# Top-32 attention and a low-rank mixer on one core: first heads masked through a gap from the scalar engine

## The chip, the cores and the metric

The kernel runs on one core of a Trainium2 chip. A core has five engines that work side by side and wait for each other through semaphores. TensorE (PE) multiplies matrices into the accumulator memory PSUM. VectorE (DVE) does elementwise work, finds the eight largest of a row (MAX8) and replaces them (MATCH_REPLACE8). ScalarE (ACT) computes a function of a scaled and shifted input. GpSimd (POOL) does elementwise work on SBUF, and SyncE (SP) issues the transfers. Each engine takes its instructions in the order of the program. The metric is the device time of one execution in microseconds, smaller being better.

## The reference

Eight batches of eight heads go through attention that keeps the 32 largest scores of each row. The result goes through a mixer with a low-rank step along the sequence and two layers along the channels.

```python
B, H, S, D = 8, 8, 576, 64            # top_k = 32
scores = (q @ k.T) / sqrt(D)
kth    = np.partition(scores, -top_k)[..., -top_k]
scores = np.where(scores >= kth, scores, -1e9)
attn   = np.exp(scores - scores.max(-1))
attn   = attn / (attn.sum(-1) + 1e-09)
x      = (attn @ v)                    # (B, S, H*D) after a transpose

h   = (x.T @ U @ V).T                  # rank 32
u   = x + h
out = u + np.maximum(u @ w_ch1, 0) @ w_ch2     # 512 -> 2048 -> 512
```

All of it is in 32-bit floats.

## The kernel before

Two heads make a pair; there are `NPAIR` = 4 pairs in a batch and 32 in all. The 576 rows of a head are four tiles of 128 rows and a tail of 64; in the tail the two heads share the 128 partitions. One tile of one pair is a step: `CH` = 5 steps to a pair and 160 steps, where step `n` is pair `g, t = divmod(n, CH)`. The first batch is the steps 0 to 19 (`ALONE` = 20). From step 20 the mixer of the batch before is fed in small pieces, `fill()`, between the steps of the attention. The mixer of the last batch comes when no attention is left.

Scores are four matmuls and copies out of PSUM. A tail takes four copies of 64 rows:

```python
S2 = attn.tile([P, 2 * (S + TAIL)], F32, tag="Ssb", bufs=3)
scs = [ps_s.tile([P, 2, 512], F32, tag="sc") for _ in range(2)]
for i, sc in enumerate(scs):
    for h in range(2):
        nc.tensor.matmul(                                              # L274
            sc[slice(0, n) if t < NT else half(h), h, 0:HALF],
            lhsT=qkT[half(h), 0, cols(t)],
            rhs=qkT[half(h), 1, i * HALF : (i + 1) * HALF], ...)
if t == NT:
    for i, sc in enumerate(scs):
        for h in range(2):
            nc.scalar.copy(S2[half(h), i*HALF : (i+1)*HALF], sc[half(h), h, 0:HALF])   # L284
    S2s[g, t] = [S2[:, 0:S]]
    return
...                                       # full tiles: three copies, L293 to L295
```

`front` is the work of a step on one tile: for each of the two heads (chunks), four times the eight largest of a row. The last of the 32 is the threshold. The first head is then masked on DVE: its exponential has been computed early, and one instruction compares with the threshold, multiplies and sums. The second head is masked on POOL before its exponential: what is below the threshold gets a huge negative number added. Each `yield` is a place where the main loop goes on with other work.

```python
order = (1, 0) if n == 2 else (0,)
for c in order:
    ms[c] = first[:, c]
    nc.vector.max(ms[c], curs[c])                                      # L320
yield
pooled = n == 2 and (g, t) != (NPAIR - 1, NT - 1)
for i in range(1, TOPK // 8):
    if i == 1:
        nc.scalar.mul(nmax[:, 0:n], first[:, 0:n, 0], -SCALE)          # L325
        for c in range(1 if pooled else n):
            weigh(chunks[c], Es[c], nmax[:, c : c + 1])                # Exp, L300
    for c in order:
        ...
        nc.vector.match_replace(nxt, ms[c], curs[c], NEG)              # L330
    for c in order:
        ...
        nc.vector.max(ms[c], curs[c])                                  # L334
    yield
if pooled:
    nc.gpsimd.tensor_scalar(Es[1], chunks[1], ms[1][:, 7:8], NEG, ALU.is_lt, ALU.mult)  # L337
    nc.gpsimd.tensor_tensor(chunks[1], chunks[1], Es[1], ALU.add)      # L338
for c in range(1 if pooled else n):
    nc.vector.scalar_tensor_tensor(out=Es[c], in0=chunks[c],           # L340
        scalar=ms[c][:, 7:8], in1=Es[c], op0=ALU.is_ge, op1=ALU.mult, accum_out=sums[c])
yield
if pooled:
    weigh(chunks[1], Es[1], nmax[:, 1:2], sums[1])                     # Exp, L300
yield
```

After this the weights E are transposed on PE (`turns`, L367 and L372, with copies `PT` on ACT) and multiplied with v (`values`, L403). The sums of a pair stand in `den`; at the pair's tail `inverse` adds 1e-9 and takes reciprocals on DVE:

```python
def inverse(g, lo, hi):
    den = dens[g][:, lo:hi]
    nc.vector.tensor_scalar_add(den, den, 1e-9)                        # L378
    nc.vector.reciprocal(den, den)                                     # L379
```

The main loop for the first batch (steps 1 to 18; at steps 19 and 20 an order of its own is used). `here` is the front of step n, whose first part has been issued, and `last` is that of step n - 1. `next_params(1)` loads one piece of the mixer's weights (36 pieces) and converts those loaded before, with three operations on ACT (L161 to L164), one on DVE (L171) and two on POOL (L172, L174); in the first batch there are six calls to a pair.

```python
next(turning, None); next(turning, None)      # rest of turns(n - 2)
scores(*divmod(n + 1, CH))
fill()
turning = turns(*divmod(n - 1, CH))
if n >= 2: values(*divmod(n - 2, CH))
next(here)                                    # i = 1
next_params(1)
next(turning, None)                           # first part of turns(n - 1)
fill()
next(last, None)                              # Exp of the second head of n - 1
next(ready, None)
next(here)                                    # i = 2
...
next(here)                                    # i = 3
if t == 1: next_params(1)
next(here)                                    # masks
fill()
```

From step 21 on:

```python
fill(); next(turning, None); fill(); next(turning, None); fill(); next(ready, None); fill()
values(*divmod(n - 2, CH)); scores(*divmod(n + 1, CH))
next(here, None)                              # i = 1
next_params(1)
...
fill(); next(here, None); fill()              # i = 2
turning = turns(*divmod(n - 1, CH)); next(turning, None)
fill(); next(here, None); next(last, None)    # i = 3; Exp of the second head of n - 1
if t in (1, 3): next_params(1)
next(here, None); fill()                      # masks
```

The pieces of the mixer that one `fill()` takes are set by a share, which is 0.91 of the full one up to step 42.

Of the kernel before, what the change touches and what calls it, by code (L numbers as in the profile page):

```python
# [8 lines left out]
F32 = mybir.dt.float32  # L9
U8 = mybir.dt.uint8  # L10
U32 = mybir.dt.uint32
AF = mybir.ActivationFunctionType
ALU = mybir.AluOpType
# [3 lines left out]


RESCALE = 2.0**-112

TINY = 0.4 * 2.0**-15

# [2 lines left out]
def kernel(  # L25
# [28 lines left out]
    nc = tc.nc  # L54
    B, H, S, D = q.shape
    P = 128
# [4 lines left out]
    NT, TAIL = 4, 64  # L61
    MAIN = NT * P
    HALF = S // 2
    assert S == MAIN + TAIL and D == 64 and H % 2 == 0 and C == 512 and TOPK % 8 == 0
    NPAIR = H // 2
# [7 lines left out]
    const = ctx.enter_context(tc.tile_pool(name="const", bufs=1))  # L73
# [37 lines left out]

    nudge = const.tile([P, 1], F32, name="nudge")
    nc.vector.memset(nudge, TINY)

    def rows(t):
        return P if t < NT else TAIL

    def cols(t):
        return slice(t * P, t * P + rows(t))
# [4 lines left out]
    def half(h):  # L124
        return slice(h * D, (h + 1) * D)
# [139 lines left out]
    def scores(g, t):  # L265


        qkT = qkTs[g]
        n = rows(t)
        S2 = attn.tile([P, 2 * (S + TAIL)], F32, tag="Ssb", name="Ssb", bufs=3)  # L270
        scs = [ps_s.tile([P, 2, 512], F32, tag="sc", name="sc") for _ in range(2)]
        for i, sc in enumerate(scs):
            for h in range(2):
                nc.tensor.matmul(  # L274
                    sc[slice(0, n) if t < NT else half(h), h, 0:HALF],
                    lhsT=qkT[half(h), 0, cols(t)],
                    rhs=qkT[half(h), 1, i * HALF : (i + 1) * HALF],
                    start=True,
                    stop=True,
                )  # L280
        if t == NT:
            for i, sc in enumerate(scs):
                for h in range(2):
                    nc.scalar.copy(  # L284
                        S2[half(h), i * HALF : (i + 1) * HALF], sc[half(h), h, 0:HALF]
                    )
            S2s[g, t] = [S2[:, 0:S]]
            return

        main = S2.rearrange("p (h n) -> p h n", h=2)  # L290
        last = S2[:, MAIN : MAIN + 2 * TAIL].rearrange("p (h n) -> p h n", h=2)
        copy = nc.vector.tensor_copy if g + t == 0 else nc.scalar.copy
        copy(main[:, :, 0:HALF], scs[0][:, :, 0:HALF])  # L293
        nc.scalar.copy(main[:, :, HALF:MAIN], scs[1][:, :, 0 : MAIN - HALF])
        nc.scalar.copy(last, scs[1][:, :, MAIN - HALF : HALF])  # L295
        S2s[g, t] = [S2[:, 0:S], S2[:, S : 2 * S]]

    def weigh(chunk, E, nmax, total=None):

        nc.scalar.activation(E, chunk, AF.Exp, bias=nmax, scale=SCALE, accum_out=total)  # L300

    def front(g, t):

        if t == 0:
            dens[g] = small.tile([P, 2 * NT + 1], F32, tag="den", name="den", bufs=3)
        chunks, den = S2s.pop((g, t)), dens[g]
        n = len(chunks)
        E2 = attn.tile([P, 2 * S], F32, tag="E", name="E", bufs=3)  # L310
        Es = [E2[:, c * S : (c + 1) * S] for c in range(n)]
        sums = [den[:, 2 * t + c : 2 * t + c + 1] for c in range(n)]
        probs[g, t] = E2
        curs, ms = list(chunks), [None] * n
        first = small.tile([P, 2, 8], F32, tag="first", name="first", bufs=3)
        nmax = small.tile([P, 2], F32, tag="nmax", name="nmax", bufs=4)
        order = (1, 0) if n == 2 else (0,)
        for c in order:
            ms[c] = first[:, c]
            nc.vector.max(ms[c], curs[c])  # L320
        yield
        pooled = n == 2 and (g, t) != (NPAIR - 1, NT - 1)
        for i in range(1, TOPK // 8):
            if i == 1:
                nc.scalar.mul(nmax[:, 0:n], first[:, 0:n, 0], -SCALE)  # L325
                for c in range(1 if pooled else n):
                    weigh(chunks[c], Es[c], nmax[:, c : c + 1])
            for c in order:
                nxt = attn.tile([P, S], F32, tag="rr", name="rr", bufs=3)
                nc.vector.match_replace(nxt, ms[c], curs[c], NEG)  # L330
                curs[c] = nxt
            for c in order:
                ms[c] = small.tile([P, 8], F32, tag="m8", name="m8", bufs=8)
                nc.vector.max(ms[c], curs[c])  # L334
            yield
        if pooled:
            nc.gpsimd.tensor_scalar(Es[1], chunks[1], ms[1][:, 7:8], NEG, ALU.is_lt, ALU.mult)  # L337
            nc.gpsimd.tensor_tensor(chunks[1], chunks[1], Es[1], ALU.add)  # L338
        for c in range(1 if pooled else n):
            nc.vector.scalar_tensor_tensor(  # L340
                out=Es[c],
                in0=chunks[c],
                scalar=ms[c][:, 7:8],
                in1=Es[c],
                op0=ALU.is_ge,
                op1=ALU.mult,
                accum_out=sums[c],
            )
        if t == NT:
            del qkTs[g]  # L350
        yield
        if pooled:
            weigh(chunks[1], Es[1], nmax[:, 1:2], sums[1])
        yield

    def turns(g, t):
# [18 lines left out]

    def inverse(g, lo, hi):
        den = dens[g][:, lo:hi]
        nc.vector.tensor_scalar_add(den, den, 1e-9)  # L378
        nc.vector.reciprocal(den, den)  # L379

    def values(g, t):
# [189 lines left out]
    for n in range(STEPS + 2):  # L571
        g, t = divmod(n, CH)
        if n < STEPS:
            if t == 0 and g + 1 < NP:
                load(g + 1)
            if t == 1 and g + 1 < NP:
                ready = prep(g + 1)
            fronts[n] = front(g, t)
            next(fronts[n])
        here, last = fronts.get(n, iter(())), fronts.pop(n - 1, iter(()))  # L580
        if n >= ALONE - 1 and n <= ALONE:

            list(turning)
            if n < ALONE:
                scores(*divmod(n + 1, CH))
            list(turns(*divmod(n - 1, CH)))
            if n < ALONE:
                values(*divmod(n - 2, CH))
                next(here)
            values(*divmod(n - 1, CH))  # L590
            if n < ALONE:
                inverse(g, 0, 2 * NT)
                next(here)
                mixing.append(mixed(g, 1))
                fill()
                next(here)
                next(here)
                continue
            fill()
            scores(*divmod(n + 1, CH))  # L600
            next(here)
            while mixing:
# [3 lines that stand above are left out]
            next(last, None)  # L606
            next(here)
            fill()
            next(here)
            next(here)  # L610
            fill()
            continue
        if n < ALONE:
            next(turning, None)
            next(turning, None)
            scores(*divmod(n + 1, CH))
            fill()
            if n >= 1:
                turning = turns(*divmod(n - 1, CH))
            if n >= 2:  # L620
                values(*divmod(n - 2, CH))
            next(here)
            next_params(1)
            next(turning, None)
            fill()
            next(last, None)
            next(ready, None)
            next(here)
            fill()
            if n >= 2 and (n - 2) % CH == NT:  # L630
                mixing.append(mixed((n - 2) // CH, 3))
            next(here)
            if t == 1:
                next_params(1)
            next(here)
            fill()
            continue
        fill()
        next(turning, None)
        fill()  # L640
        next(turning, None)
# [3 lines that stand above are left out]
        if n - 2 >= ALONE:  # L645
            values(*divmod(n - 2, CH))
        if n + 1 < STEPS:
            scores(*divmod(n + 1, CH))
        next(here, None)
        next_params(1)  # L650
        if n - 2 >= ALONE and (n - 2) % CH == NT:
            mixing.append(mixed((n - 2) // CH, 4))
        fill()
        next(here, None)
        fill()
        if n <= STEPS:
            turning = turns(*divmod(n - 1, CH))
        next(turning, None)
        fill()
        next(here, None)  # L660
        next(last, None)
        if t in (1, 3):
            next_params(1)
        next(here, None)
        fill()
# [33 lines left out]
```

## Time and profile before

| | |
|---|---|
| time | 1860.22 us, median of 3 runs (1859.81 to 1860.23) |
| span of the profiled run | 1861.6 us |
| PE busy | 1750.6 us, 94% |
| DVE busy | 1617.2 us, 87% |
| ACT busy | 1008.1 us, 54% |
| POOL busy | 635.7 us, 34% |

These shares are averages over a run with different stages, so they don't tell what a change in one stage is worth. The page also has the busy tenths of each engine in 40 equal slices, the groups of instructions by line, and the chain of work that ended last. The trace behind it answers for any stretch of time what each engine did and what it waited for.

### The profile page before, as it was taken

What the parts mean: (1) busy time and instruction counts of PE and PEld (TensorE: products, weight loads), DVE (VectorE), ACT (ScalarE), POOL (GpSimd) and SP (SyncE); (2) the same over time, 40 slices, a digit from 0 to 9 for tenths busy, and PEclk for the clock granted to TensorE, in tenths of its full rate; (3) what the DMA queues carried; (4) which work ended last, traced back from release to release, by engine and by line L of the source; (5) the groups of instructions that cost most, each with busy time, mean ns of one, the idle gap of its engine ahead of it and who ended that gap; (6) DMA issues with size and microseconds to landing.
All of it is one profiled execution on the core that took longest, in us unless ns stands there. A gap on an engine that the chain in (4) does not pass through costs nothing.

```text
span 1861.6 us, 29241 instructions
## 1 busy us (share of the span) xinstructions
PE 1750.6 (94%) x10528; PEld 1324.0 (71%) x10528; DVE 1617.2 (87%) x3316; ACT 1008.1 (54%) x2466; POOL 635.7 (34%) x432
## 2 busy tenths in 40 slices
PE   4565789999999999999999999999999999999999
PEld 3443556787777877788777877788777877788677
DVE  7999999999999999999999999999999999996000
ACT  4666677555655555555555555555555555554111
POOL 4556466433333332323233332332323332322000
PEclk7677799999999999999999999999999999999999
DMA  3222222101000010110001010101001010000000
GB/s 98 76 72 75 63 81 81 28 23 32 15 21 22 23 29 21 30 25 24 23 13 31 21 32 20 28 22 27 14 24 27 25 30 21 10 8 7 6 14 12
DMA packets 127296, 58.23 MB, mean 31 GB/s; under 512 B 89904, under 2 KB 124976, under 8 KB 127152
## 3 DMA queue, kind: packets, MB, share of 16 engines
q1 hardware_dynamic: 126096, 56.10, 11.3%
q8 instruction: 84, 1.38, 0.3%
q14 instruction: 60, 0.49, 0.1%
q10 hardware_dynamic: 1056, 0.26, 0.1%
HBM read 46.89 MB, written 9.44 MB: 30 GB/s over the span
## 4 chain that ended last, share of the span: by engine, by line
PE 84%; DVE 10%; ACT 4%; issue 1%; POOL 1%; DMA 0%; POOLq 0%; SPq 0%; DVEq 0%; ACTq 0%
PE mm L472 27%; PE mm L491 26%; PE sc L274 9%; PE O L403 6%; PE tp L367 6%; DVE rr L330 4%; DVE m L334 3%; PE O L390 2%; PE up L447 2%; PE O L400 1%; DVE first L320 1%; PE tp L254 1%; PE tp L519 1%; PE up L449 1%; PE tp L372 1%
## 5 line engine op out<-in xcount | busy, mean ns | idle before, releaser
L334 DVE MAX8 m<-rr 128x8 f32<-128x576 f32 x864 | 614.8, 749 | 5.5
L491 PE MATMUL mm<-hT,w 128*128 128x256 f32 (+1 forms) x2048 | 562.2, 410 | 0.0
L472 PE MATMUL mm<-uT,w 128*128 128x256 f32 (+1 forms) x2048 | 557.9, 411 | 1.5 <-ACT hT L484 1.5
L337 POOL TENSOR_SCALAR E<-Ssb,m 128x576 f32<-128x576 f32 x127 | 285.2, 2246 | 650.7 <-DVE m L334 512.7
L472 PEld LDWEIGHTS mm<-uT,w 128*128 128x128 f32 x2048 | 363.3, 190 | 108.6 <-issue 27.6
L491 PEld LDWEIGHTS mm<-hT,w 128*128 128x128 f32 x2048 | 360.5, 190 | 97.7 <-issue 22.5
L330 DVE MATCH_REPLACE8 rr<-m,rr 128x576 f32<-128x576 f32 x576 | 427.8, 743 | 0.0
L367 PE MATMUL tp<-ident,E 128*128 128x128 f32 x1152 | 184.7, 285 | 53.8 <-ACT E L300 38.7
L368 ACT COPY PT<-tp 128x512 f32<-128x512 f32 x288 | 168.4, 585 | 114.9 <-PE tp L367 113.0
L300 ACT ACTIVATE E<-Ssb,nmax 128x576 f32<-128x576 f32 x288 | 223.8, 778 | 5.9 <-POOL Ssb L338 0.7
L367 PEld LDWEIGHTS tp<-ident,E 128*128 128x128 f32 x1152 | 144.9, 147 | 106.9 <-ACT E L300 50.7
L274 PE MATMUL sc<-qkT 64*128 64x288 f32 (+1 forms) x1280 | 212.5, 454 | 0.3 <-ACT Ssb L293 0.3
L330 DVE MATCH_REPLACE8 rr<-first,Ssb 128x576 f32<-128x576 f32 x288 | 211.8, 742 | 0.0
L320 DVE MAX8 first<-Ssb 128x8 f32<-128x576 f32 x288 | 205.4, 750 | 0.9 <-ACT Ssb L295 0.9
L340 DVE SCALAR_TENSOR_TENSOR E<-Ssb,m,E 128x576 f32<-128x576 f32 x161 | 137.8, 856 | 65.6 <-ACT E L300 48.2
L338 POOL TENSOR_TENSOR Ssb<-Ssb,E 128x576 f32<-128x576 f32 x127 | 178.9, 1408 | 10.6
L484 ACT ACTIVATE hT<-mm 128x320 f32<-128x320 f32 (+1 forms) x256 | 104.4, 408 | 119.8 <-PE mm L472 119.0
L412 ACT COPY XT<-O 128x128 f32<-128x128 f32 x128 | 34.0, 266 | 215.1 <-PE O L403 215.1
L403 PE MATMUL O<-PT,va 128*64 128x128 f32 x2048 | 147.7, 289 | 0.0
L274 PEld LDWEIGHTS sc<-qkT 64*128 64x128 f32 (+1 forms) x1280 | 110.2, 187 | 51.7 <-issue 25.4
L504 DVE TENSOR_TENSOR oT<-uT,mm 128x320 f32<-128x320 f32 (+1 forms) x8 | 3.6, 455 | 146.6 <-PE mm L491 146.6
L403 PEld LDWEIGHTS O<-PT,va 128*64 128x64 f32 x2048 | 116.0, 143 | 16.8 <-issue 2.9
(73 smaller groups left out, 1484.3 us busy)
## 6 DMA issues: line engine op xcount, KB each, us to landing
raw<-in_moe_w_ch_dram SPq DMA_DIRECT2D x32, 512.0 KB, 3.7
va<-in_v_dram SPq DMA_DIRECT2D x64, 128.0 KB, 2.5
out_dram<-ob SPq DMA_DIRECT2D x64, 128.0 KB, 1.9
ld_q<-in_q_dram SPq DMA_DIRECT2D x63, 128.0 KB, 2.8
ld_k<-in_k_dram SPq DMA_DIRECT2D x63, 128.0 KB, 2.8
ld_ends<-in_q_dram SPq DMA_DIRECT2D x32, 32.0 KB, 2.2
ld_ends<-in_k_dram SPq DMA_DIRECT2D x32, 32.0 KB, 2.2
vd<-in_v_dram SPq DMA_DIRECT2D x64, 16.0 KB, 2.0
```

What stands on the lines that cost most here:

```text
L274: nc.tensor.matmul(sc[slice(0, n) if t < NT else half(h), h, 0:HALF], lhsT=qkT[half(h), 0, cols(t)], rhs=qkT[half(h), 1, i * HALF : (i + 1 ...
L300: nc.scalar.activation(E, chunk, AF.Exp, bias=nmax, scale=SCALE, accum_out=total)
L320: nc.vector.max(ms[c], curs[c])
L330: nc.vector.match_replace(nxt, ms[c], curs[c], NEG)
L334: nc.vector.max(ms[c], curs[c])
L337: nc.gpsimd.tensor_scalar(Es[1], chunks[1], ms[1][:, 7:8], NEG, ALU.is_lt, ALU.mult)
L338: nc.gpsimd.tensor_tensor(chunks[1], chunks[1], Es[1], ALU.add)
L367: nc.tensor.transpose(tp[:, j, :], E2[:, a : a + P], ident)
L368: nc.scalar.copy(PT[:, NT * h : NT * h + NT], tp)
L403: nc.tensor.matmul(O[half(h)], lhsT=va[:, h, j, :], rhs=PT[:, NT * h + j], start=False, stop=(j == NT - 1),)
L472: nc.tensor.matmul(ph[:, 0:w], lhsT=w1[:, cc, f * P : (f + 1) * P], rhs=uT[:, cc, lo:hi], start=(cc == 0), stop=(cc == NC - 1),)
L491: nc.tensor.matmul(po[:, 0:w], lhsT=w2[:, f, c * P : (c + 1) * P], rhs=hTs[f][:, 0:w], start=(f == 0), stop=(f == NF - 1),)
```

## The change

It has four parts. *First*, in the first two batches (`eased`: pairs 0 to 7, full tiles, all but tile 3 of pair 3) the first head no longer gets its mask on DVE. ACT computes, for every score, Relu of (threshold - score) x 2^96: zero for a score that is kept, a huge gap for one that is not. POOL subtracts this from the scores, and the exponential, which is then taken after the mask and no longer early, makes zero of what fell out. ACT and POOL do this at the head of the next step. *Second*, as the weights of a step are ready later, the main loop of the first batch takes the values three steps behind and the transposes a place later, and the calls for weights are spread otherwise, still six to a pair. *Third*, the addition of 1e-9 goes from DVE to ACT, for all pairs but pair 3. *Fourth*, the tail's four score matmuls go into one PSUM tile, which one copy empties. The aim is to take work off DVE while it is fully used, and to shorten ACT's part of the tails.

```diff
+WIDEN = 2.0**96
 ...
+        if t == NT:
+            sc = ps_s.tile([P, 2, 512], F32, tag="sc", name="sc")
+            for i in range(2):
+                for h in range(2):
+                    nc.tensor.matmul(sc[half(h), i, 0:HALF], ...)
+            nc.scalar.copy(S2[:, 0:S].rearrange("p (i n) -> p i n", i=2), sc[:, :, 0:HALF])
+            S2s[g, t] = [S2[:, 0:S]]
+            return
 ...
+    def eased(g, t):
+        return g < 2 * NPAIR and t < NT and (g, t) != (NPAIR - 1, NT - 1)
 ...
+        ease = eased(g, t)
         pooled = n == 2 and (g, t) != (NPAIR - 1, NT - 1)
+        early = range(0 if ease else 1 if pooled else n)
 ...
-                for c in range(1 if pooled else n):
+                for c in early:
                     weigh(chunks[c], Es[c], nmax[:, c : c + 1])
 ...
-        for c in range(1 if pooled else n):
+        for c in early:
             nc.vector.scalar_tensor_tensor(...)
         yield
-        if pooled:
-            weigh(chunks[1], Es[1], nmax[:, 1:2], sums[1])
+        if ease:
+            least = small.tile([P, 1], F32, tag="least", name="least", bufs=3)
+            nc.scalar.mul(least, ms[0][:, 7:8], WIDEN)
+            nc.scalar.activation(Es[0], chunks[0], AF.Relu, bias=least, scale=-WIDEN)
+            nc.gpsimd.tensor_tensor(chunks[0], chunks[0], Es[0], ALU.subtract)
+            yield
+        for c in order:
+            if c not in early:
+                weigh(chunks[c], Es[c], nmax[:, c : c + 1], sums[c])
+        if t == NT and g != NPAIR - 1:
+            nc.scalar.activation(den, den, AF.Identity, bias=eps)
         yield
 ...
-        nc.vector.tensor_scalar_add(den, den, 1e-9)
+        if g == NPAIR - 1:
+            nc.vector.tensor_scalar_add(den, den, 1e-9)
 ...                                          # first batch, steps 1 to 18
-            next(turning, None)
-            next(turning, None)
+            if ease:
+                next(last, None)              # gap and subtraction of n - 1
             scores(*divmod(n + 1, CH))
-            fill()
-            if n >= 1:
-                turning = turns(*divmod(n - 1, CH))
-            if n >= 2:
-                values(*divmod(n - 2, CH))
-            next(here)
-            next_params(1)
-            next(turning, None)
-            fill()
-            next(last, None)
+            if n >= 3:
+                values(*divmod(n - 3, CH))
+            list(turning)                     # all of turns(n - 2)
+            fill()
+            next(here)
+            if t < NT:
+                next_params(1)
+            fill()
             next(ready, None)
             next(here)
+            next(last, None)                  # Exp of both heads of n - 1
             ...
-            if t == 1:
+            if t in (0, 1):
                 next_params(1)
             next(here)
             fill()
+            if n >= 1:
+                turning = turns(*divmod(n - 1, CH))
 ...                                          # from step 21 on
+        if ease:
+            next(last, None)                  # gap and subtraction of n - 1, ahead of all else
         ...
             scores(*divmod(n + 1, CH))
         next(here, None)
+        if ease:
+            next(last, None)                  # Exp of both heads of n - 1
         next_params(1)
```

At step 19 the values of steps 16, 17 and 18 are taken, where before it was those of 17 and 18.

## The prediction

> **What bounds the kernel now.** I read the page's slices first, because the program has stages with different limits, then busy times cut at step boundaries, then the cost groups, then the DVE's timeline.
>
> ```profile
> PE   4565789999999999999999999999999999999999
> DVE  7999999999999999999999999999999999996000
> PEclk7677799999999999999999999999999999999999
> ```
>
> One digit is 46.5 us. For five slices DVE is full while PE is at half and its clock below full; then both are full until slice 36; at the end PE runs alone. So there are three stages. I cut them at the first MAX8 of each step: step 20, where the second batch begins and the first mixer layer starts to run, has it at 223.94 us, step 40 at 434.46, and the last DVE work of the attention ends near 1707.6. The columns are stretch, its length, then busy time with the instruction count for each engine, clock, DMA share, GB/s.
>
> ```profile
> 114.93:168.05 53.12, 32.63 (x201) 22.32 (x201) 52.04 (x111) 35.62 (x81) 31.60 (x21) 0.79 0.27 77
> 223.94:434.46 210.52, 201.29 (x1238) 148.68 (x1237) 204.91 (x425) 138.99 (x330) 106.46 (x70) 1.00 0.18 50
> 434.46:1707.60 1273.14, 1265.40 (x7865) 966.46 (x7864) 1200.61 (x2452) 709.95 (x1767) 411.84 (x263) 1.00 0.09 23
> 1707.60:1861.60 154.00, 148.64 (x667) 117.50 (x665) 3.64 (x8) 23.19 (x61) 3.21 (x4) 1.00 0.04 11
> ```
>
> The first row is one pair of heads (five steps) of batch 0: DVE 52.04 of 53.12 us, PE 32.63. Batch 0 is DVE-bound. The second is batch 1: DVE 204.91 and PE 201.29 of 210.52, both near the limit, PE with 9.23 us idle. From step 40 PE is busy 1265.40 of 1273.14 us: there PE is the bound and DVE's gaps cost nothing. The last row is PE alone. A DVE instruction is therefore worth its time in batch 0, a part of it in batch 1, and nothing later.
>
> Next the groups that the change touches (line, engine, operation, count | busy us, mean ns | idle before it).
>
> ```profile
> L340 DVE SCALAR_TENSOR_TENSOR E<-Ssb,m,E 128x576 f32<-128x576 f32 x161 | 137.8, 856 | 65.6 <-ACT E L300 48.2 <-PE tp L367 1.3 <-ACT hT L484 0.5
> L378 DVE TENSOR_SCALAR den<-den 128x9 f32<-128x9 f32 (+2 forms) x33 | 25.9, 786 | 0.3 <-ACT E L300 0.3
> L337 POOL TENSOR_SCALAR E<-Ssb,m 128x576 f32<-128x576 f32 x127 | 285.2, 2246 | 650.7 <-DVE m L334 512.7 <-PE tp L367 57.3 <-PE mm L472 40.0
> L338 POOL TENSOR_TENSOR Ssb<-Ssb,E 128x576 f32<-128x576 f32 x127 | 178.9, 1408 | 10.6
> L300 ACT ACTIVATE E<-Ssb,nmax 128x576 f32<-128x576 f32 x288 | 223.8, 778 | 5.9 <-POOL Ssb L338 0.7
> L284 ACT COPY Ssb<-sc 64x288 f32<-64x288 f32 x128 | 50.3, 393 | 15.9 <-PE sc L274 14.7
> L293 ACT COPY Ssb<-sc 128x576 f32<-128x576 f32 x127 | 81.2, 639 | 48.4 <-PE sc L274 46.8
> ```
>
> What is to be seen: the mask of a first head costs DVE 856 ns, POOL's second-head mask 2246 + 1408 ns, and a nine-column add to `den` 786 ns, more than a MAX8 over 576 columns. How much a mask really takes out of a DVE step is in the timeline, as start, duration, instruction.
>
> ```profile
> 180.59 1.02 DVE L378 TENSOR_SCALAR den<-den 128x9 f32<-128x9 f32 x1
> 181.64 0.22 DVE L379 RECIPROCAL den<-den 128x9 f32<-128x9 f32 x1
> ...
> 233.10 1.41 DVE L334 MAX8 m<-rr 128x8 f32<-128x576 f32 x2
> 234.65 0.82 DVE L340 SCALAR_TENSOR_TENSOR E<-Ssb,m,E 128x576 f32<-128x576 f32 x1
> 235.39 0.08 DVE L340 DVE_READ_ACCUMULATOR E<-Ssb,m,E 128x1 f32 x1
> 235.39 1.42 DVE L320 MAX8 first<-Ssb 128x8 f32<-128x576 f32 x2
> ```
>
> Two MAX8 that end a pass are followed elsewhere 1.33 us after their start; here the next MAX8 starts 2.29 us after (235.39 - 233.10). The mask costs 0.96 us of the step. The add costs 1.05 us (181.64 - 180.59).
>
> **What the Trainium skill says.** "SBUF — State Buffer", section "Who interferes with whom", says that GpSimd's only SBUF ports are the DVE's second pair, that a DVE tensor_scalar in a two-port mode takes the pair as an exclusive lock, and that a DVE operation with two SBUF inputs contends with GpSimd's reads. The trace agrees: the add takes from 134 to 1057 ns for nine columns or fewer and the mask from 809 to 1666 ns for one shape. MAX8 has one input, and stays between 735 and 764 ns, so more POOL work should not stretch it. "ScalarE: Activation LUTs", section "What ACT_TABLE_LOAD costs", gives an ACTIVATE with a pointer bias as 280 ns + 0.833 ns per element, by which I estimate 760 ns for the new Relu over 576 columns; the Exp of the same shape and bias measures 778 ns here, and I use that. Its section "Table sets: the hidden batching unit" has Relu in every set; the trace has one table load although Relu and Exp alternate, so no reload is to be paid. "Perfetto Trace Analysis", section "Optimizing Scalar/DVE Operations", advises fewer, larger operations because each pays a fixed access cost: four tail copies take 4 x 393 = 1572 ns, one copy of 128x576 takes 639.
>
> **The change, part by part.**
>
> *Masks leave DVE in the first two batches.* Of the 16 full tiles of batch 0 all but (3, 3) are eased: 15 x 0.96 = 14.4 us; in some steps a weight conversion stands just ahead of the mask and the mask adds only 0.73 us (190.97 to 191.70), so I take 13.7 us. Batch 1: 16 x 0.96 = 15.4 us.
>
> *The add of 1e-9 leaves DVE* for all pairs but 3. In batch 0 three of them fall (pairs 0 to 2): 3 x 1.05 = 3.1 us. In batch 1 four: 4.2 us. Later ones fall where PE is the bound: nothing.
>
> *What comes in.* ACT per eased tile: `least` (0.2 us, as `nmax`, 217 ns), Relu 0.78, and the accumulator read that the first head's Exp now has, 0.19: 1.2 us. Per pair 4 x 1.2, less 0.93 for the tail's copies, plus 0.2 for the add: 4 us. ACT goes from 35.6 to about 39.7 of a pair that shrinks to 53.1 - 4 x 0.91 - 1.05 = 48.4 us, 82%. POOL: 4 x 1.41 = 5.6, from 31.6 to 37.2, 77%. Neither fills, but both work in order, and POOL's chain for one tile is now 2.25 + 1.41 + 1.41 = 5.1 us, then two Exps of 0.97. It starts when the second head's last MAX8 is done, 0.75 us before the step ends; so both heads' E are ready some 6 us into the next step, up to 10 where two conversions (2 x 2.7 us on POOL) stand ahead. In batch 0 PE transposes E(n-1) only in step n+1 now, which leaves room; that is what the values three steps behind are for. The scores of step n+1 are copied right after the Relu and are wanted 10 us later. So I expect no new wait on DVE there.
>
> *Batch 0:* 13.7 + 3.1 = 16.8 us, all on the path.
>
> *Batch 1:* DVE's need falls from about 210.5 to 210.5 - 15.4 - 4.2 = 191 us, below PE's 201.3, which the change leaves as it is (the matmuls and the pace of the mixer's pieces per step are the same). PE becomes the bound. It could win at most its 9.2 idle us. But here E(n-1) is still transposed in the middle of step n, about 7 to 8 us in by the timeline, and in the first two pairs conversions delay POOL; ACT, which then sits at the two Exps, holds back the copies that PE's banks wait for. I put 2.5 us for that: 6.7 us won.
>
> *Tails in one copy:* 0.93 us of ACT in each of 32 tails, and one score buffer less. DVE waited 0.9 us in all for score copies to begin MAX8 and PE 0.3 us for score buffers, so it is worth nothing by itself.
>
> *Sum:* 16.8 + 6.7 = 23.5; 1860.2 - 23.5 = 1836.7, say 1837 us.
>
> **The rivals.**
>
> *A: the gain of batch 0 alone.* The late E of batch 1 makes new PE waits as long as the idle time it replaces. For it: between 230 and 480 us PE already waits 4.9 us for E by the waits, with a shorter chain. Against: PE behind DVE makes E early, not late. Time: 1860 - 17 = 1843.
>
> *B: POOL and ACT become the bound in batch 0.* ACT at 82% and POOL at 77%, in order, each waiting for the other and for weights; a stall of the Exp would reach DVE through the next scores. For it: two conversions now fall in each of the first two steps of a pair, and ACT's work there about fills a step. Against: some 7 us of slack before DVE needs a score tile. Loss of a third of the 16.8: about 1843, with rival A 1849.
>
> *C: everything comes, and more.* PE's idle time in batch 1 goes entirely, and the 3.6 us of idle at the start of batch 2, which came from a POOL add waiting behind a mask, goes with it: 16.8 + 9.2 + 3.6 = 29.6, 1831.
>
> *D: the den add matters in the long stage.* PE's 7.7 us of idle from step 40 on caps it, and that idle is not DVE's doing. I give it little.
>
> **Range and chances.** The batch 0 part is counting of instructions on a full engine and should hold within 3 us; batch 1 is open between 0 and 9 us. The range goes from just beyond C, 1829, to A with B, 1849. Faster by over 2% would need 1823 us, 37 us less, and all DVE time removed in both batches is 36.4: 4%. Slower by over 2% would need a bound in the long stage, whose instructions hardly change: 2%. Within 2%: 94%.
>
> **What would show it.** In the changed profile: step 20 begins near 207 us instead of 223.94; DVE at 96% or more of batch 0, with pairs of about 48.4 us; 130 masks of the old kind on DVE instead of 161; PE above 98% busy in the stretch of steps 20 to 39, which lasts about 204 us; the stretch from step 40 to the end as long as now, 1427 us, within 3. It is wrong if step 20 begins after 212 (then ACT or POOL has held DVE: rival B), if batch 1 lasts more than 208 us (rival A), or if the stretch after step 40 has changed by over 5 us, for which I have no mechanism.

## The result, and the profile after

The changed kernel takes 1867.35 us, median of 4 runs (1867.0 to 1867.74), against 1860.22 us before (1859.81 to 1861.27): ratio 1.0038, 95% interval 1.002 to 1.0055. It is slower by 7 us, where the prediction had 1837 us and a range from 1829 to 1849.

The first view is again the page's slices, of the kernel after.

```profile
PE   4665789999999999999999999999999999999999
DVE  7999988888999999999999999999999989996000
```

DVE has a row of 8s from slice 6 to 10, that is from about 233 to 466 us, where it had 9s. It has been relieved there, and the run didn't get shorter. Cut at step boundaries, step 20 now begins at 212.96 us and step 40 at 437.57. The rows are the pairs 1 to 3 of batch 0, all of batch 1, one pair of batch 1, and the stretch after it up to 1707.60 us; columns as before.

```profile
59.53:212.96 153.43, 96.33 (x621) 66.04 (x621) 147.38 (x306) 114.08 (x269) 104.53 (x72) 0.78 0.28 80
212.96:437.57 224.61, 202.55 (x1217) 147.29 (x1216) 189.97 (x387) 145.78 (x362) 122.93 (x83) 0.98 0.16 44
326.90:383.77 56.87, 53.02 (x321) 39.41 (x321) 46.02 (x94) 31.62 (x86) 23.55 (x16) 0.97 0.10 26
437.57:1707.60 1270.03, 1263.82 (x7864) 965.92 (x7865) 1183.87 (x2423) 690.73 (x1719) 413.77 (x264) 1.00 0.09 22
```

Batch 1 is where the time went: 224.61 us instead of 210.52. DVE's busy time there fell from 204.91 to 189.97 us, PE's is 202.55, and PE is idle for 22.1 us instead of 9.2. From step 40 to the end it is 1428.3 us against 1427.1, unchanged. Batch 0 gives 11.0 us instead of 16.8 in these two profiles.

One correction belongs here: the profiled run of the kernel before took 1863.4 us, 3 more than its median, and has 2.2 us of waiting at step 19 that a run of usual length doesn't have (experiment 9). Against that run, step 20 at 221.71, batch 0 gives 8.75 us.

The groups that answer to those shown before:

```profile
L359 DVE SCALAR_TENSOR_TENSOR E<-Ssb,m,E 128x576 f32<-128x576 f32 x130 | 117.1, 901 | 93.5 <-ACT E L310 83.0 <-PE tp L548 0.5
L310 ACT ACTIVATE E<-Ssb,nmax 128x576 f32<-128x576 f32 x288 | 222.2, 775 | 14.3 <-POOL Ssb L357 6.2 <-POOL Ssb L375 3.9
L375 POOL TENSOR_TENSOR Ssb<-Ssb,E 128x576 f32<-128x576 f32 x31 | 44.4, 1433 | 9.7 <-ACT E L374 9.5
L374 ACT ACTIVATE E<-Ssb,least 128x576 f32<-128x576 f32 x31 | 24.0, 775 | 1.0
L286 ACT COPY Ssb<-sc 128x576 f32<-128x576 f32 x32 | 20.4, 637 | 25.1 <-PE sc L279 25.1
```

31 masks have left DVE, the Relu takes 775 ns, the subtraction 1433, the tail's one copy 637: every added piece has the size that the prediction gave it. New is the idle time: DVE's remaining masks wait 83 us for the exponential, 48 before.

What PE waits for in batch 1 stands in the waits (who waited for whom: us in total, times, longest). First the kernel before, in its run of usual length, then the kernel after.

```profile
PE tp L367 <- ACT E L300: 4.9, 5, 1.8
```

```profile
PE tp L395 <- ACT E L310: 13.3, 15, 2.5
```

PE's transposes wait for the exponential in nearly every one of the 16 full tiles. One such place in the timeline of the kernel after (start, duration, engine, instruction, idle before), from the last link of POOL's chain for the tile that is then transposed:

```profile
354.42 1.42 POOL L375 TENSOR_TENSOR Ssb<-Ssb,E 128x576 f32<-128x576 f32 x1
...
359.71 1.24 PE L292 MATMUL sc<-qkT 64*128 64x288 f32 x8
...
360.51 0.64 ACT L303 COPY Ssb<-sc 128x576 f32<-128x576 f32 x1 [0.42 <-PE sc L292]
360.88 1.56 PE L501 MATMUL mm<-uT,w 128*128 128x256 f32 x6
361.05 0.54 ACT L304 COPY Ssb<-sc 128x448 f32<-128x448 f32 x1
361.47 0.28 ACT L305 COPY Ssb<-sc 128x128 f32<-128x128 f32 x1
361.63 0.23 ACT L344 ACTIVATE nmax<-first 128x2 f32<-128x2 f32 x1
361.73 0.79 ACT L310 ACTIVATE E<-Ssb,nmax 128x576 f32<-128x576 f32 x1
361.79 1.42 DVE L337 MAX8 first<-Ssb 128x8 f32<-128x576 f32 x2 [3.32 <-ACT Ssb L305]
...
362.49 0.78 ACT L310 ACTIVATE E<-Ssb,nmax 128x576 f32<-128x576 f32 x1
...
363.42 0.66 PE L395 MATMUL tp<-ident,E 128*128 128x128 f32 x4 [0.97 <-ACT E L310]
```

POOL was done at 355.84. The exponentials started 5.9 us later, because they stand on ACT behind the copies of the next scores, and those wait for PE's own score matmuls. PE then has only the 1.56 us of mixer matmuls (L501) before it needs the result, and waits 0.97 us. However far PE lags, the exponential lags with it. Meanwhile DVE, which is ahead, stands 3.32 us for scores. In 12 of the 16 tiles of batch 1 the first exponential starts 2.2 to 5.9 us after POOL's last subtraction; in the other four, all in the first two pairs, POOL was done 0.7 us or less before it, or not yet.

### The profile page after: what moved, and what is told of

Same layout as the page of the kernel before. It is cut to its first block, busy times and chain, and to the rows that moved or that the text cites. A ratio compares the mean times of both kernels' runs of the same rounds, so it can differ in the third digit from the quotient of the medians.

```text
span 1865.9 us, 29142 instructions
## 1 busy us (share of the span) xinstructions
PE 1747.5 (94%) x10528; PEld 1319.3 (71%) x10528; DVE 1576.7 (85%) x3224; ACT 1009.2 (54%) x2494; POOL 675.0 (36%) x463
## 4 chain that ended last, share of the span: by engine, by line
PE 84%; DVE 6%; ACT 4%; POOL 3%; issue 2%; DMA 0%; POOLq 0%; SPq 0%; DVEq 0%; ACTq 0%
PE mm L501 26%; PE mm L520 26%; PE sc L292 7%; PE O L432 6%; PE tp L395 6%; DVE rr L349 3%; DVE m L353 2%; PE up L476 2%; PE sc L279 2%; PE O L419 2%; ACT E L310 2%; PE O L429 1%; PE tp L258 1%; PE up L478 1%; PE tp L548 1%
## 5 line engine op out<-in xcount | busy, mean ns | idle before, releaser
L501 PE MATMUL mm<-uT,w 128*128 128x256 f32 (+1 forms) x2048 | 557.8, 411 | 0.5 <-ACT hT L513 0.5
L501 PEld LDWEIGHTS mm<-uT,w 128*128 128x128 f32 x2048 | 363.9, 190 | 107.4 <-issue 28.0
L395 PE MATMUL tp<-ident,E 128*128 128x128 f32 x1152 | 179.3, 280 | 47.5 <-ACT E L310 24.2
L395 PEld LDWEIGHTS tp<-ident,E 128*128 128x128 f32 x1152 | 140.5, 143 | 102.6 <-ACT E L310 39.7
L359 DVE SCALAR_TENSOR_TENSOR E<-Ssb,m,E 128x576 f32<-128x576 f32 x130 | 117.1, 901 | 93.5 <-ACT E L310 83.0
L292 PE MATMUL sc<-qkT 64*128 64x288 f32 x1024 | 169.6, 452 | 8.4 <-ACT Ssb L303 7.9
L432 PE MATMUL O<-PT,va 128*64 128x128 f32 x2048 | 143.7, 284 | 0.0
L536 POOL TENSOR_TENSOR oT<-oT,uT 128x320 f32<-128x320 f32 (+1 forms) x56 | 45.1, 806 | 230.9 <-ACT oT L535 230.9
L292 PEld LDWEIGHTS sc<-qkT 64*128 64x128 f32 x1024 | 93.0, 197 | 46.1 <-issue 16.6
```

The costliest lines, as they stand in the source:

```text
L292: nc.tensor.matmul(sc[:, h, 0:HALF], lhsT=qkT[half(h), 0, cols(t)], rhs=qkT[half(h), 1, i * HALF : (i + 1) * HALF], start=True, stop=True,)
L395: nc.tensor.transpose(tp[:, j, :], E2[:, a : a + P], ident)
L432: nc.tensor.matmul(O[half(h)], lhsT=va[:, h, j, :], rhs=PT[:, NT * h + j], start=False, stop=(j == NT - 1),)
L501: nc.tensor.matmul(ph[:, 0:w], lhsT=w1[:, cc, f * P : (f + 1) * P], rhs=uT[:, cc, lo:hi], start=(cc == 0), stop=(cc == NC - 1),)
```

## The experiments

Theory A: batch 1 loses through the place of the exponentials in ACT's order. Rival C: through POOL's chain, which has become longer by a subtraction. Rival B: through a part that all stages share. Theory D: the rest of batch 0's gain is lost in the weights' conversion on DVE, which waits for the port that POOL holds. Theory F came later: through the place of the tail's own exponential on ACT.

**1. Gap masks in the first batch only.**

```diff
-        return g < 2 * NPAIR and t < NT and (g, t) != (NPAIR - 1, NT - 1)
+        return g < NPAIR and t < NT and (g, t) != (NPAIR - 1, NT - 1)
```

> The changed kernel with the gap masks in the first batch only (pairs 0 to 3); the second batch masks its first heads on VectorE as before. Theory A (the loss is made in the second batch, where the two exponentials now stand behind the next scores' copies on the scalar engine, ahead of the transposes that need them): steps 20 to 39 last about 210 us as in the kernel before, the 11 us won in the first batch stay, total about 1850 us (1847 to 1853). Rival B (the loss comes from a part that all stages share, the tails' single copy or the addition on the scalar engine): total stays near 1865.

Measured: 1850.43 us (ratio to before 0.9947, 0.993 to 0.9963). Steps 20 to 39 last 210.84 us. The second batch's gap masks cost 17 us; rival B falls.

**2. The first head's exponential first.**

```diff
-        for c in order:
+        for c in range(n):
             if c not in early:
```

> The changed kernel with the two exponentials in the other order: the first head, which is transposed first, goes first. Theory A (order on the scalar engine): the first head's weights come one exponential, 0.97 us, earlier in 16 tiles of the second batch, TensorE's waits for them there fall from 13.3 us to under 5, total about 1858 us (1854 to 1861). Rival C (GpSimd's chain of three operations is what is waited for; the first head's subtraction is its last link): no gain, 1865 to 1869.

Measured: 1861.43 us (1.0001, 0.9992 to 1.0009), just above the expected range. PE's waits for the weights in batch 1 fall from 13.3 to 5.4 us, the stretch from 224.61 to 217.09. The edit also turns the order in batch 0, where step 20 begins at 214.81 us, 1.9 later. One exponential of 0.97 us earlier is worth 6 us on balance: order on ACT, not POOL, whose first-head subtraction is still the last link.

**3. Both exponentials ahead of the next scores.**

```diff
         fill()
+        if ease:
+            next(last, None)
         if n - 2 >= ALONE:
             values(*divmod(n - 2, CH))
         if n + 1 < STEPS:
             scores(*divmod(n + 1, CH))
         next(here, None)
-        if ease:
-            next(last, None)
```

> The changed kernel with both exponentials of the step before issued ahead of the values and the scores of the next step in the second batch, not behind them. Theory A: TensorE's waits for the weights in steps 20 to 39 nearly vanish (under 3 us), the stretch shrinks from 224.6 to 205-209 us, total 1848 to 1854 us. Rival C (GpSimd's chain): the scalar engine now stands at the exponentials until GpSimd is done and the score copies come later; the stretch grows, total over 1868.

Measured: 1852.82 us (0.9959, 0.9944 to 0.9974). The waits fall to 3.3 us. The stretch, 211.73 us, stays above the 205 to 209 expected. Its four pairs, from the busy times:

```profile
212.33:268.08 55.75, 48.18 (x278) 33.25 (x278) 50.18 (x104) 41.69 (x99) 39.06 (x27) 1.00 0.25 74
268.08:323.75 55.67, 50.79 (x300) 36.00 (x299) 48.71 (x100) 40.88 (x98) 38.06 (x27) 0.97 0.20 58
323.75:374.19 50.44, 50.44 (x322) 38.68 (x321) 45.74 (x94) 32.04 (x86) 22.77 (x15) 0.99 0.11 29
374.19:424.06 49.87, 49.87 (x332) 40.88 (x331) 45.62 (x94) 31.36 (x83) 21.71 (x14) 1.00 0.10 22
```

The last two are full of PE work, as predicted. In the first two, where POOL still converts weights (39 us of 56, against 22 of 50), PE is idle 12.5 us and DVE waits 10.8 us in the two tails for the exponential. There rival C has a part: ACT stood up to 2.9 us for POOL at the moved exponentials.

**4. The gap subtracted twice in the second batch.**

```diff
-            nc.gpsimd.tensor_tensor(chunks[0], chunks[0], Es[0], ALU.subtract)
+            for _ in range(2 if g >= NPAIR else 1):
+                nc.gpsimd.tensor_tensor(chunks[0], chunks[0], Es[0], ALU.subtract)
```

> The changed kernel with the gap subtracted twice on GpSimd in the second batch, so that GpSimd's chain for a tile is 1.4 us longer; the result is the same since the gap is zero for a kept score. Theory A: the chain is done before the exponentials' turn comes, total within 4 us of the changed kernel (1865 to 1871). Rival C (GpSimd's chain is waited for): up to 16 x 1.4 = 22 us more, total 1880 to 1890.

Measured: 1869.99 us (1.005, 1.0035 to 1.0065), 2.6 us more than the changed kernel for some 22 us of POOL work added to its chain. In the changed kernel, rival C is left with little.

**5. No gap masks at all, the rest of the change kept.**

```diff
-        return g < 2 * NPAIR and t < NT and (g, t) != (NPAIR - 1, NT - 1)
+        return False
```

> The changed kernel without any gap mask (VectorE masks every first head as before); the other loop order in the first batch, the addition on the scalar engine and the tails' single copy stay. If the gap masks make all of batch 0's gain but the three additions (3 us), step 20 begins near 221 us and the total is 1856 to 1859 us. Rival: the other order by itself gains or costs more than 3 us, total outside 1854 to 1862.

Measured: 1858.01 us (0.9986, 0.9979 to 0.9993), step 20 at 219.74 us. With experiment 1 this gives the first batch's gap masks 1858.0 - 1850.4 = 7.6 us for 13.7 us of DVE time.

**6. The tails' single copy alone, on the kernel before** (the tail's branch of `scores` from the diff above).

> The kernel before with the tails' single tile and copy alone. Theory: 30 us less work on the scalar engine that nothing waits for; total within 2 us of 1860. Rival: in the long stage TensorE gets the score buffers and VectorE the tails sooner, 1 us or more in each of the 32 pairs, total below 1840.

Measured: 1859.33 us (0.9991, 0.9982 to 0.9999). The medians differ by 0.7 us, and the interval allows 0.2 to 3.3.

**7. The addition of 1e-9 on ACT alone, on the kernel before** (`eps`, the Identity activation, and the condition in `inverse` from the diff above).

> The kernel before with the addition of 1e-9 on the scalar engine alone. Theory: three additions of 1.05 us fall on the full VectorE of batch 0, so step 20 begins 3 us sooner; the later ones fall where TensorE is the bound; total 1856 to 1858 us. Rival: VectorE is worth something in the long stage too, 25 us less work there, total below 1850.

Measured: 1853.66 us (0.9959, 0.9945 to 0.9973), below the expected range: this part of the change alone is worth 6 us, twice what was expected. Against the run of experiment 9, step 20 begins 3.3 us sooner (218.43), as counted, and from there to the end the run is 2.7 us shorter. Experiment 5 has this part too, with the single copy and the other loop order of the first batch, and is 4.3 us slower. Only 1.3 us of that stand in the first batch (step 20 at 219.74 instead of 218.43). The rest comes later, mostly in batch 1 (210.52 us instead of 208.34), where the tails of its first two pairs wait 4.4 us for their exponential; what makes those waits was not tried apart.

**8. The first call for weights one pass later**, on the kernel of experiment 1.

```diff
             next(here)
-            if t < NT:
-                next_params(1)
             fill()
             next(ready, None)
             next(here)
+            if t < NT:
+                next_params(1)
             next(last, None)
```

> The kernel with gap masks in the first batch only, with the first call for weights of a step in that batch one pass later, so that its conversion on VectorE stands some 7 us into the step, not 4, when GpSimd's chain for the step before is done. Theory D (the rest of batch 0's gain was lost as the conversion waits for the port that GpSimd holds: 19 conversions of 590 ns on average instead of 407): their mean falls back under 450 ns, step 20 begins 2 to 4 us sooner than 212.1, total 1846 to 1848 us. Rival E (the loss is elsewhere): no change from 1850.4.

Measured: 1854.99 us (0.9967, 0.9954 to 0.998), step 20 at 215.70: worse by 3.6 us in batch 0. The expectation fails, as the conversions' mean is 651 ns, not under 450. The steps t = 3 became short (10.23 us for 10.98), but the steps t = 1 and 2 long (11.37 for 10.75 and 11.05 for 10.30): the call had been moved into POOL's work of other steps. DVE's waits in tails also rose from 3.3 to 5.9 us.

**9. The kernel before once more.**

> The kernel before once more, for its profile: the profiled run shown so far took 1863.4 us, 3 more than its median. If those 3 us are the 2.2 us wait of VectorE at step 19 and the waits in the tail of step 29, which the profiles of the tails alone and of the addition alone don't have, step 20 begins near 222 us and steps 20 to 39 last 208 to 209 us when the run takes 1860; otherwise 224 and 210.5 as shown.

Measured: 1860.29 us; the profiled run took 1859.52. Step 20 begins at 221.71 us, as expected; steps 20 to 39 last 210.36, not 208 to 209. Only the wait at step 19 was peculiar to the first profile.

**10. The call of the steps t = 3 behind the last MAX8**, on the kernel of experiment 1.

```diff
-            if t < NT:
+            if t < 3:
                 next_params(1)
 ...
-            if t in (0, 1):
+            if t in (0, 1, 3):
                 next_params(1)
```

> The kernel with gap masks in the first batch only, with the call for weights of the steps t = 3 in that batch moved behind the last MAX8, where GpSimd's chain of the step before is over. Theory D (the conversion waits for the port that GpSimd holds): each step t = 3 shrinks from 10.97 to about 10.24 us, step 20 begins about 3 us sooner than 212.1, total about 1847.5 us. Rival E: GpSimd's next chain now starts later and the tails wait as much longer; total 1850 or more.

Measured: 1849.73 us (0.9943, 0.9928 to 0.9958), step 20 at 212.75. First what D says of the conversions (the group of batch 0, the changed kernel and then this one):

```profile
L175 DVE TENSOR_SCALAR w<-w 128x512 uint32<-128x512 uint32 x19 | 11.2, 590 | 0.0
```

```profile
L175 DVE TENSOR_SCALAR w<-w 128x512 uint32<-128x512 uint32 x19 | 8.2, 434 | 0.0
```

The steps t = 3 of the first three pairs take 10.22 us to the hundredth. So D is right that the conversions take longer beside POOL's chain (that the port is the reason, no run shows apart), and E about the sum: against experiment 1 the tails behind them grew from 6.82 to 8.42 and from 7.56 to 9.79 us, and nothing was won. Something else holds the tails.

A part of it is the clock that PE is granted (1.00 is full speed), which changes within batch 0. Two pairs of runs have the very same program up to step 20. The tail of the third pair, as stretches of the changed kernel and of experiment 1, then of experiments 10 and 11 (the clock is the third number from the end):

```profile
151.55:160.72 9.17, 8.75 (x57) 6.15 (x55) 6.24 (x14) 5.74 (x15) 4.58 (x3) 0.71 0.11 43
151.66:159.22 7.56, 7.16 (x57) 4.70 (x55) 6.23 (x12) 5.66 (x15) 4.59 (x3) 0.89 0.15 57
151.37:161.16 9.79, 9.30 (x59) 6.57 (x57) 6.25 (x14) 5.63 (x14) 7.53 (x5) 0.70 0.18 54
151.81:160.23 8.42, 7.57 (x65) 5.19 (x61) 7.22 (x14) 6.02 (x14) 7.55 (x5) 0.96 0.21 63
```

In the first two, 57 matmuls take 8.75 us at a clock of 0.71 and 7.16 at 0.89. The same tail lasts 1.4 to 1.6 us longer at the lower clock, so single tails of two runs can't be compared without it.

**11. The same, and in the later batches the second call of a pair at t = 0.**

```diff
-        if t in (1, 3):
+        if t in (0, 1):
             next_params(1)
```

> The same, and in the later batches the second call for weights of a pair goes from the steps t = 3 to t = 0, so that no conversions stand ahead of GpSimd's mask before a tail. If the long tails of the first two pairs of the second batch (9.6 and 8.6 us instead of 7) come from these conversions, steps 20 to 39 shrink from 210.8 to 206-208 us and the total is 1844 to 1846 us; if not, as the kernel with the call at the end.

Measured: 1849.51 us (0.9942, 0.9926 to 0.9959); steps 20 to 39 last 210.45 us. The tails of the first two pairs are still 8.54 and 9.26 us. The conversions ahead of them are not the cause.

What holds a tail stands in the timeline of the changed kernel, in the tail of batch 0 that lasts 9.17 us:

```profile
155.27 0.27 ACT L441 COPY XT<-O 128x128 f32<-128x128 f32 x1 [1.47 <-PE O L432]
156.31 0.59 ACT L396 COPY PT<-tp 128x512 f32<-128x512 f32 x1 [0.77 <-PE tp L395]
...
158.92 0.21 ACT L344 ACTIVATE nmax<-first 128x1 f32<-128x1 f32 x1
159.16 1.44 ACT L310 ACTIVATE E<-Ssb,nmax 128x576 f32<-128x576 f32 x2
...
159.97 0.82 DVE L359 SCALAR_TENSOR_TENSOR E<-Ssb,m,E 128x576 f32<-128x576 f32 x1 [2.65 <-ACT E L310]
```

The tail's own early exponential needs only the first MAX8, over at 152.3, but on ACT it comes behind the copies of values and transposes, for which ACT waits on PE. In the new order all transposes of a tile are taken at once there. So the wait grows with the time that PE takes: the tail of the second pair, at a clock of 1.00, waits only 0.32 us. This is theory F, the same fault as in batch 1.

**12. The tail's exponential at the head of its step**, in the first two batches, on the kernel of experiment 11.

```diff
             scores(*divmod(n + 1, CH))
+            if t == NT:
+                next(here)
             if n >= 3:
                 values(*divmod(n - 3, CH))
             list(turning)
             fill()
-            next(here)
+            if t < NT:
+                next(here)
 ...                                          # from step 21 on
+        ahead = t == NT and n < 2 * ALONE
+        if ahead:
+            next(here, None)
         fill()
         next(turning, None)
 ...
-        next(here, None)
+        if not ahead:
+            next(here, None)
```

> The kernel with gap masks in the first batch only and the calls moved at both ends, and with the tail's own exponential of the first two batches issued at the head of its step, ahead of the copies of transposes and values. Theory F (VectorE's waits in tails come from the exponential's place on the scalar engine, behind copies that TensorE releases): the waits for it fall from 3.9 us in batch 0 and about 4 in batch 1 to under 1 each, step 20 begins near 208 us instead of 211.7, steps 20 to 39 last 207 to 209 us, total 1843 to 1846 us. Rival: TensorE itself is late, the waits move to the next step's scores; total 1848 or more.

Measured: 1845.53 us (0.992, 0.9905 to 0.9935). DVE's waits for the exponential, in batch 0 of this kernel:

```profile
DVE E L359 <- ACT E L310: 0.2, 1, 0.2
```

They were 3.9 us before this edit, and fall from there to 0.2, and the tails of the second and third pair last 7.03 and 7.05 us at clocks of 0.76 and 0.84. Step 20 begins at 208.39 us instead of 211.67: for batch 0, F holds in the size expected. In batch 1 the waits fall from 4.6 to 1.0 us, and steps 20 to 39 last 208.57 us, but from step 20 to the end the run takes 1635.9 us, against 1636.0 in experiment 11 and 1635.9 in the kernel before (experiment 9). There the edit wins nothing: step 40 is DVE's mark, and what PE has not done by then it does after it.

**13. The same with gap masks in the second batch too, exponentials ahead of the scores** (the edit of experiment 1 undone, that of experiment 3 made).

> The same with the gap masks in the second batch too, and their exponentials ahead of the next scores. If the second batch is bound by TensorE once no exponential stands in a bad place, steps 20 to 39 last 203 to 206 us as the prediction had it, total 1840 to 1844; if GpSimd's longer chain and the scalar engine's load in the first two pairs hold it up, 208 us or more and no gain over the kernel with gap masks in the first batch only.

Measured: 1845.15 us (0.9917, 0.99 to 0.9933). The stretch and its last two pairs:

```profile
209.07:415.70 206.63, 196.30 (x1217) 146.13 (x1217) 192.33 (x389) 145.18 (x363) 122.39 (x83) 1.00 0.17 48
315.11:415.70 100.59, 100.39 (x651) 79.19 (x650) 91.63 (x187) 63.22 (x168) 45.70 (x30) 1.00 0.11 26
```

206.63 us lies between the two expectations. It is 2 us less than in experiment 12 for 15 us of DVE time, and the difference of the total is inside the spread of the runs. In the last two pairs PE is busy 100.39 of 100.59 us, so nothing is left there. The exponentials now hold back the score copies instead, for which DVE waits 8.5 us in the stretch. Experiments 12 and 13 are 0.8% faster than the kernel before and 1.2% faster than the changed one.

## Why the prediction was wrong

*Where the bound lies:* right for batch 0, which is DVE's, and for the long stage, which is PE's: from step 40 on DVE is busy 14.4 us less (1204.25 and 1189.81), and the stretch is 1 us longer. That PE becomes the bound of batch 1 did not come about; it is idle for 22.1 us there.

*Sizes of the added work:* right, as the groups show. For DVE's need in batch 1 the prediction took 19.6 us off the length of the stretch, 210.5, and came to 191. The like measure is the stretch less DVE's waits in it, and that went from 209.2 to 192.2 us.

*Batch 1:* this step failed. The prediction said of rival A that "PE behind DVE makes E early, not late", took 2.5 us for the late E and won 6.7; the stretch lost 14.1. It saw that the chain on POOL gets longer, and measured E's time from the end of DVE's step. But the exponential's start was set by its place in ACT's queue, behind score copies that PE itself releases; its lead over PE's transposes is fixed in program order, and being early with the data is no help. Experiment 2 (one exponential earlier, 6 us), 3 (both ahead, 14.5 us) and 4 (POOL longer, 2.6 us) show it. That ACT "holds back the copies" was named in the prediction, but in the changed kernel it was the other way round: the copies held back the exponential. PE waits 2.6 us for copies of `PT` there, against 1.1 before, and 13.3 us for E, against 4.9. Even with the order mended (experiment 13), batch 1 lasts not 204 us but 206.6, and from step 20 to the end 1634.1 us, 1.8 less than in the kernel before, where 6.7 were predicted. PE's work there is what was counted (1613.0 us busy, 1615.3 before). What did not go away with DVE relieved is PE's idle time: 10.1 us of it stand in the first two pairs. Of it, 4.7 us are waits of the mixer's first matmuls for the scaled values from POOL; the rest was not tried.

*Batch 0:* the sum of 16.8 us was over by 8 against a run of usual length. Two terms were missing. The trace's own example of the port, the addition to `den`, was used for that instruction alone, though the weights' conversion is an instruction of the same kind; 23 of them took 12.8 us instead of 8.3 for 22, of which one call more is 0.4. Half of it comes from the new places of the calls alone: in experiment 5, without gap masks, the 23 take 10.8 us. "SBUF — State Buffer", section "Who interferes with whom", in the Trainium skill, says that a tensor_scalar in a two-port mode and a GpSimd instruction shut each other out, the first issued going first, and the trace agrees that they collide: 0.41 us alone and 1.16 where a POOL operation was under way. And the tails wait 4.3 us, where the run of usual length has no such wait: the sentence "I expect no new wait on DVE there" looked at the score copies and not at the tail's exponential, which the new loop order had put behind more PE work. (Experiment 5 has this order without gap masks and no such wait, but its tails ran at a clock of 1.00, so it doesn't tell the two apart.) 4.1 + 4.3 = 8.4. Experiment 10 takes away most of the first and 12 the second; with both gone, step 20 begins at 208.39 us, 13.3 us sooner than in the run of usual length. What is left to 16.8 is 3.5 us, and by the lengths of the instructions it lies in two places, though no run takes it away. The 23 conversions still take 9.9 us, where the 22 took 8.3. And the six masks left in batch 0, which took 4.9 us in the changed kernel, take 7.0 in experiment 12:

```profile
L359 DVE SCALAR_TENSOR_TENSOR E<-Ssb,m,E 128x576 f32<-128x576 f32 x6 | 4.8, 817 | 4.5 <-ACT E L310 4.3
```

```profile
L359 DVE SCALAR_TENSOR_TENSOR E<-Ssb,m,E 128x576 f32<-128x576 f32 x6 | 7.0, 1175 | 0.6 <-ACT E L310 0.2
```

*The addition on ACT:* its 3.1 us in batch 0 are confirmed (3.3). Alone it also won 2.7 us after step 20. In the changed kernel it brings a wait of its own: DVE's reciprocals stand 2.2 us in batch 1 for the addition on ACT.

*The single copy:* 0.7 us alone by the medians, where nothing was predicted.

*The rivals:* A named the cause, the late E of batch 1, but as a loss no larger than the idle time that stood there, and answered it with the sentence that failed. B named ACT and POOL in batch 0, and a stall of the exponential that reaches DVE through the next scores; the stall came in the tails, through the mask. D was small, C did not come. Two of the signs of being wrong came true: step 20 begins at 212.96 us (after 212), and batch 1 lasts 224.61 (more than 208).

## What to carry to other kernels

When work moves from the bounding engine to another, ask not only whether that engine has time, but behind what it will stand in that engine's order, and who releases that. A consumer that waits for a result queued behind its own output can't be helped by slack: PE's score matmuls released the exponential that PE then waited for. After moving an operation, put its place in the queue right first, and judge the size afterwards: the same masks cost 17 us in one order and nothing in another.

## What the hardware showed that was not expected

A DVE tensor_scalar over 128x512 32-bit words takes 0.41 us by itself; issued at 144.66 us, 0.2 us after the start of a POOL tensor_tensor of 1.06, it took 1.16. The masks, with two inputs in SBUF, take 818 ns as a rule; in experiment 12, where POOL's work had moved beside them, those of the first three tails took 1186 to 1207 ns and that of the second head of pair 3, tile 3, 1841. POOL's subtractions beside the three tails took 1926 ns, where their mean was 1433 in the changed kernel. And the addition of a constant to nine columns, 1.02 us for so little data, was worth 6 us of 1860 when it left DVE in 31 places (experiment 7). The same tail of batch 0 lasted 7.56 us at a granted clock of 0.89 (experiment 1) and 9.17 us at 0.71 (the changed kernel), while DVE was busy 6.23 and 6.24 us of it.
